# Loading q and k as whole tokens and transposing them on VectorE in an attention and two-MLP kernel

## The chip, the cores and the metric

The kernel runs on one core of a Trainium2 chip. The metric is the device time of one execution in microseconds (us), from three timed runs and one profiled execution. A core has a matrix engine (PE; PEld is its weight load), a vector engine (DVE), a scalar engine (ACT), a general engine (POOL) and a queue engine (SP) that issues the transfers here.

## The reference

```python
scores = scale * np.matmul(q, k.transpose(0, 1, 3, 2))    # 4 batches, 8 heads, 576 tokens, 64 features
masks = [mask_plain if h < H // 2 else mask_dil for h in range(H)]
scores = np.where(masks[None], scores, -1e9)
attn = exp(scores - max) / (sum + 1e-9)
x = matmul(attn, v)                                       # then to (4 * 576) tokens x 512
h = x @ w_in;  x = np.maximum(0.01 * h, h) @ w_out        # 512 -> 2048 -> 512
a = x @ w1;  b = x @ w2;  out = ((a * b) @ w3) @ w_out2    # 512 -> 1024 -> 1024 -> 512
```

The plain mask of heads 0 to 3 keeps the last 32 keys, the dilated one of heads 4 to 7 every fourth of the last 128. The weights are double precision.

## The kernel before

**Work and tiles.** Heads are taken in pairs, four a batch, two dilated and then two plain; a pair's work is cut into two parts r, so there are 32 steps n of attention. `x` of a batch feeds the first MLP in chunks c of 320 and 256 tokens: `hidden(c, f)` multiplies by the weight block `win` f into PSUM (`ps_h`), ACT takes the leaky unit (`g`), DVE and POOL or DVE split the result in a high and a low half (`gs`), and `project` multiplies by `wout` f into `ps_x`, two turns f later (`LAG = 2`). Each product is three matmuls (`mm3`, L112 to L114). After chunk 4 comes a folding of the last two weight matrices, and at the end the gated layer (`ps_ab`) and the output (`ps_y`).

**Weights.** While batch 0's attention runs, 32 blocks of double precision weights (`raw0` to `raw31`, win and wout in turn) are fetched by SP and converted by POOL (L103), ACT (L143, L145) and DVE (L146, L147), and split (L107, L108). Block 26 makes win 13.

**q and k.** `load_qk(m)` fetches q (m even) or k (m odd) of a pair: two transfers (L244), one for each head, with 6 (plain) or 8 (dilated) tokens a partition on 96 or 72 partitions, so that the two heads of a token stand side by side in pieces of 64 features, 256 bytes each. `transpose_qk(m)` turns the tile with 6 or 8 PE transposes (L306) in two groups of 3 or 4, each group into one PSUM bank, and DVE copies each bank to `qT` (L309, with the scale) or `kT` (L311) in the order of tokens that the masks want. `scores(n)` multiplies blocks of 64 queries by 96 keys (L328), DVE adds the mask (L336) and takes the maximum (L338), ACT the exponential (L341); `normalize`, `transpose_p` (L371) and `values` (L389) follow.

**Buffers.** Tiles of batch 0 (m below 8) have memory of their own in the place of weights; from batch 1 on all q and k tiles share the tag `nat` with two buffers, so a load waits until the tile two before it has been turned. `qT` and `kT` have two buffers each. Scores, values and the transposes of later batches share two PSUM banks (`side_bank`).

**Order.** A scheduler orders the instructions of each engine from the program's order and its own estimate of times; SP's order is kept by hand while the weights are fetched. `attention` calls, in step n, `transpose_p(n)`, `normalize(n+1)`, `scores(n+2)`, `transpose_qk(n+4)`, `load_qk(n+6)`, `values(n)`; `pace` interleaves these steps with the turns of the MLP.

Of the kernel before, what the change touches and what calls it, by code (L numbers as in the profile page):

```python
# [8 lines left out]
F32 = mybir.dt.float32  # L9
# [8 lines left out]
ALU = mybir.AluOpType  # L18
# [4 lines left out]
DILATION = 4  # L23
# [5 lines left out]
def tile_window_attention_two_mlps(  # L29
# [14 lines left out]
    nc = tc.nc  # L44
    P = 128
    B, H, S, D = q.shape
    T, DM = out.shape
    F1 = w_in.shape[1]
    F2 = w1.shape[1]
    SCALE = 1.0 / float(D) ** 0.5  # L50
    NC = DM // P
    NF = F1 // P
# [7 lines left out]
    SR = S // DILATION  # L60
# [4 lines left out]
    HP = H // 2  # L65


    def pool(name, side):
        es = ExitStack()
        return es, es.enter_context(  # L70
            tc.tile_pool(name=name, bufs=1, side=side, reuse_waits="tile")
        )
# [3 lines left out]
    win_es, win_p = pool("win", "left")  # L76
# [11 lines left out]
    def side_bank(name):  # L88
        return psum.tile([P, 512], F32, tag="side", name=name, bufs=2)

    def bank(name):
        return psum.tile([P, 512], F32, tag="h", name=name, bufs=2)
# [26 lines left out]
    def rows(t, off, dims):  # L119
        return bass.AP(t.tensor, t.offset + off, dims)  # L120
# [67 lines left out]
    win, wout, w12, wo2, wp = {}, {}, {}, {}, {}  # L188
# [26 lines left out]
    nat_t, v_t, qk_t, xs = {}, {}, {}, {}  # L215


    order, seq = [], []
# [7 lines left out]
    def pair(pi):  # L226
        b, h0 = divmod(pi, HP)
        return b, 2 * h0, 2 * h0 < H // 2

    def load_qk(m):  # L230
        if m >= 2 * NPAIR:
            return
        pi, nm = seq[m // 2], "qk"[m % 2]
        b, h0, plain = pair(pi)
        c = 6 if plain else 8
        n = S // c
        if m < 2 * HP:
            t = win_p.tile([P, 8, 2, D], F32, tag="win", name=f"{nm}{pi}", bufs=NF)
        else:
            t = att.tile([P, 8, 2, D], F32, tag="nat", name=f"{nm}{pi}", bufs=2)  # L240
        src = q if nm == "q" else k
        o = (b * H + h0) * S * D
        for j in range(2):
            nc.sync.dma_start(  # L244
                t[:n, :c, j, :], rows(src, o + j * S * D, [[c * D, n], [D, c], [1, D]])
            )
        nat_t[nm, pi] = t
# [5 lines left out]
    def first_key(i, plain):  # L253
        k0 = max(i * QB - WINDOW, 0)
        g0 = i * QB // SR * SR
        return k0 if plain else max(k0, g0)
# [31 lines left out]
    def transpose_qk(m):  # L288

        if m >= 2 * NPAIR:  # L290
            return
        pi, nm = seq[m // 2], "qk"[m % 2]
        plain = pair(pi)[2]
        c = 6 if plain else 8
        n = S // c
        t = nat_t.pop((nm, pi))
        dst = att.tile([P, S], F32, tag=nm + "T", name=f"{nm}T{pi}", bufs=2)
        if plain:
            to = dst.rearrange("d (p g c) -> d g c p", g=2, p=n)
        else:  # L300
            to = dst.rearrange("d (c p g) -> d g c p", g=2, p=n)
        for g in range(2):
            ps = (bank if m < 2 * HP else side_bank)(f"ps_{nm}T{pi}_{g}")
            for c1 in range(c // 2):
                src = t[:n, g * (c // 2) + c1].rearrange("p j d -> p (j d)")
                nc.tensor.transpose(ps[:, c1 * n : (c1 + 1) * n], src, ident[:n, :n])  # L306
            src = ps[:, : S // 2].rearrange("d (c p) -> d c p", p=n)
            if nm == "q":
                nc.vector.tensor_scalar(to[:, g], src, SCALE, None, op0=ALU.mult)  # L309
            else:  # L310
                nc.vector.tensor_copy(to[:, g], src)  # L311
        qk_t[nm, pi] = dst

    sm = {}
# [1 line left out]
    def scores(n):  # L316
        if n >= NR:
            return
        pi, r = order[n]
        plain = pair(pi)[2]  # L320
        qt, kt = qk_t["q", pi], qk_t["k", pi]
        bl = R_BLOCKS[r]
        nb = len(bl)
        ps = side_bank(f"ps_s{n}")[:, : nb * KB].rearrange("p (i k) -> p i k", k=KB)
        for i in bl:
            for j in range(2):
                d = slice(j * D, (j + 1) * D)
                nc.tensor.matmul(  # L328
                    ps[j * QB : (j + 1) * QB, i - bl.start],
                    qt[d, i * QB : (i + 1) * QB],  # L330
                    kt[d, first_key(i, plain) : first_key(i, plain) + KB],
                    start=True, stop=True,
                )
        s = att.tile([P, NQ, KB], F32, tag="s", name=f"s{n}", bufs=3)[:, :nb]
        mk = mask_p[:, NQ - nb :] if plain else mask_d[:, bl.start : bl.stop]
        nc.vector.tensor_tensor(s, ps, mk, op=ALU.add)  # L336
        nmax = att.tile([P, NQ], F32, tag="nmax", name=f"nmax{n}", bufs=2)
        nc.vector.tensor_reduce(nmax[:, :nb], s, op=ALU.max, axis=AX.X, negate=True)  # L338
        total = att.tile([P, NQ], F32, tag="total", name=f"total{n}", bufs=2)
        for i in range(nb):  # L340
            nc.scalar.activation(  # L341
                s[:, i], s[:, i], AF.Exp, bias=nmax[:, i : i + 1], accum_out=total[:, i : i + 1]
            )
        sm[n] = (s, total[:, :nb])
# [84 lines left out]
    def attention(n0, n1):  # L429

        for n in range(n0, n1):
            if n == N_EARLY:
                for m in range(NA, NA + 2):
                    load_qk(m)
                load_v(4)
                for m in range(NA, n + 4):
                    transpose_qk(m)
                    load_qk(m + 2)
                load_v(5)
# [3 lines left out]
            if n % 8 != 3:  # L443
                scores(n + 2)
                yield
            if n >= N_EARLY or n + 4 < NA:
                transpose_qk(n + 4)
            if n >= N_EARLY:
                load_qk(n + 6)
            yield  # L450
            if n % 8 == 3:
                scores(n + 2)
                yield
# [186 lines left out]
    with ExitStack():  # L640
        make_identity(nc, ident)
        att_es, att = pool("att", "right")
# [54 lines left out]
        with tc.manual_schedule(engines={mybir.EngineType.SP}):  # L697


            first = attention(0, N_EARLY)  # L700
            for x in "0aM1bFF2cFF3dFFFFXAAAAAAAAAAAACCCCCCCC":
                if x in "0123":
                    load_qk(2 * int(x))
                    load_qk(2 * int(x) + 1)
                elif x in "abcd":
                    load_v("abcd".index(x))
                elif x == "M":
                    build_masks()
                elif x == "X":
                    transpose_qk(0)  # L710
                    transpose_qk(1)
                    scores(0)
                    scores(1)
                    transpose_qk(2)
                    normalize(0)
                    transpose_qk(3)
                elif x == "A":
                    step(first, first)
                elif x == "F":
                    conv.fetch()  # L720
                else:
                    conv.step()
            step(*[first] * 10)
# [169 lines left out]
```

## Time and profile before

| what | value |
|---|---|
| timed runs | 916.11, 917.04, 918.66 us; median 917.04 |
| span of the profiled execution, first to last instruction | 916.2 us (no other time of that execution is given; its span lies 0.8 us under the median of the runs) |
| busy PE, DVE, ACT, POOL | 880.8, 345.9, 354.5, 247.8 us |
| transfers | 110938 packets, 95.94 MB |

The page gives busy time per engine, the span in 40 slices, the chain of work that ended last, and groups of instructions by line. A share of the whole span mixes stages: up to about 113 us weights are converted, from 113 to 355 us the PE transposes of q and k run between matmuls of the first MLP, and later stages have none of them. So the sums are made from windows and from the order of time.

### The profile page before, as it was taken

What the parts mean: (1) busy time and instruction counts of PE and PEld (TensorE: products, weight loads), DVE (VectorE), ACT (ScalarE), POOL (GpSimd) and SP (SyncE); (2) the same over time, 40 slices, a digit from 0 to 9 for tenths busy, and PEclk for the clock granted to TensorE, in tenths of its full rate; (3) what the DMA queues carried; (4) which work ended last, traced back from release to release, by engine and by line L of the source; (5) the groups of instructions that cost most, each with busy time, mean ns of one, the idle gap of its engine ahead of it and who ended that gap; (6) DMA issues with size and microseconds to landing.
All of it is one profiled execution on the core that took longest, in us unless ns stands there. A gap on an engine that the chain in (4) does not pass through costs nothing.

```text
span 916.2 us, 16026 instructions
## 1 busy us (share of the span) xinstructions
PE 880.8 (96%) x6456; PEld 832.4 (91%) x6456; DVE 345.9 (38%) x699; ACT 354.5 (39%) x904; POOL 247.8 (27%) x288
## 2 busy tenths in 40 slices
PE   4869899999999999999999999999999999999998
PEld 4658799999999999999999999999999998999997
DVE  4999864444333233264334345851101010100000
ACT  3898742433333333365333245742212121211211
POOL 3454410012222223254222143432213031211110
PEclk9559999999999999999999999999999999999999
DMA  7995502322213102177788665620101010000000
GB/s 170 313 271 129 180 19 57 83 48 73 49 44 78 45 14 62 47 252 282 235 293 271 211 201 160 202 79 1 46 24 35 35 35 24 12 24 12 12 24 35
DMA packets 110938, 95.94 MB, mean 105 GB/s; under 512 B 69520, under 2 KB 94352, under 8 KB 110864
## 3 DMA queue, kind: packets, MB, share of 16 engines
q1 hardware_dynamic: 110864, 94.92, 34.8%
q8 instruction: 51, 0.84, 0.4%
q14 instruction: 23, 0.19, 0.1%
HBM read 78.51 MB, written 16.38 MB: 104 GB/s over the span
## 4 chain that ended last, share of the span: by engine, by line
PE 82%; DVE 6%; ACT 3%; DMA 3%; SPq 2%; issue 2%; POOL 1%; DVEq 0%; POOLq 0%; ACTq 0%
PE ps_ab L112 7%; PE ps_ab L114 7%; PE ps_ab L113 7%; PE ps_h L113 6%; PE ps_h L114 6%; PE ps_x L112 6%; PE ps_h L112 6%; PE ps_x L114 6%; PE ps_x L113 6%; PE ps_y L113 4%; PE ps_y L112 4%; PE ps_y L114 4%; PE ps_s L328 2%; PE ps_o L389 2%; PE ps_wp L114 2%
## 5 line engine op out<-in xcount | busy, mean ns | idle before, releaser
L112 PE MATMUL ps_h<-x,win 128*128 128x320 f32 (+1 forms) x512 | 154.7, 303 | 3.6 <-DMA v<-in_v_dram 2.3
L113 PE MATMUL ps_h<-x,win 128*128 128x320 f32 (+1 forms) x512 | 155.4, 304 | 1.1 <-DVE x L422 1.1
L113 PE MATMUL ps_x<-gs,wout 128*128 128x320 f32 (+1 forms) x512 | 152.8, 299 | 2.4 <-DVE gs L108 2.4
L114 PE MATMUL ps_h<-x,win 128*128 128x320 f32 (+1 forms) x512 | 154.4, 302 | 0.0
L112 PE MATMUL ps_x<-gs,wout 128*128 128x320 f32 (+1 forms) x512 | 152.1, 299 | 1.1 <-DVE x L509 1.1
L114 PE MATMUL ps_x<-gs,wout 128*128 128x320 f32 (+1 forms) x512 | 152.7, 299 | 0.0
L112 PE MATMUL ps_ab<-ys,w 128*128 128x384 f32 x384 | 130.1, 339 | 0.0
L114 PE MATMUL ps_ab<-ys,w 128*128 128x384 f32 x384 | 130.0, 339 | 0.0
L113 PE MATMUL ps_ab<-ys,w 128*128 128x384 f32 x384 | 130.0, 338 | 0.0
L616 DVE TENSOR_TENSOR ab<-a,ps_ab 128x384 f32<-128x384 f32 x48 | 26.6, 554 | 253.0 <-ACT a L614 247.9
L107 DVE CAST gs<-g 128x320 fp32r<-128x320 f32 (+1 forms) x128 | 49.7, 391 | 153.6 <-ACT g L473 153.4
L108 POOL TENSOR_TENSOR p<-ab,p 128x384 fp32r<-128x384 f32 x48 | 48.5, 1011 | 218.6 <-ACT p L107 218.6
L108 POOL TENSOR_TENSOR gs<-g,gs 128x320 fp32r<-128x320 f32 (+1 forms) x80 | 66.4, 831 | 145.2 <-DVE gs L107 145.2
L112 PEld LDWEIGHTS ps_h<-x,win 128*128 128x128 f32 x512 | 97.9, 192 | 5.3 <-ACT x L420 4.2
L113 PEld LDWEIGHTS ps_x<-gs,wout 128*128 128x128 f32 x512 | 96.9, 189 | 3.8 <-DVE gs L108 2.9
L113 PEld LDWEIGHTS ps_h<-x,win 128*128 128x128 f32 x512 | 98.3, 192 | 2.1 <-DVE x L422 1.3
L112 PEld LDWEIGHTS ps_x<-gs,wout 128*128 128x128 f32 x512 | 96.5, 189 | 2.6 <-DVE x L509 1.3
L114 PEld LDWEIGHTS ps_h<-x,win 128*128 128x128 f32 x512 | 98.4, 192 | 0.3
L114 PEld LDWEIGHTS ps_x<-gs,wout 128*128 128x128 f32 x512 | 96.9, 189 | 0.5
L473 ACT ACTIVATE g<-ps_h 128x320 f32<-128x320 f32 (+1 forms) x128 | 51.4, 403 | 115.2 <-PE ps_h L114 114.1
L614 ACT COPY a<-ps_ab 128x384 f32<-128x384 f32 x48 | 23.0, 480 | 143.9 <-PE ps_ab L114 143.9
L112 PEld LDWEIGHTS ps_ab<-ys,w 128*128 128x128 f32 x384 | 72.0, 188 | 1.2
(91 smaller groups left out, 1514.8 us busy)
## 6 DMA issues: line engine op xcount, KB each, us to landing
wo<-wo_dram SPq DMA_DIRECT2D x32, 512.0 KB
raw<-in_moe_w_in_dram SPq DMA_DIRECT2D x16, 512.0 KB
raw<-in_moe_w_out_dram SPq DMA_DIRECT2D x16, 512.0 KB
rawf<-in_moe_w_dram SPq DMA_DIRECT2D x16, 512.0 KB
raww<-in_moe_w_dram SPq DMA_DIRECT2D x16, 512.0 KB
v<-in_v_dram SPq DMA_DIRECT2D x60, 96.0 KB
q<-in_q_dram SPq DMA_DIRECT2D x32, 144.0 KB
k<-in_k_dram SPq DMA_DIRECT2D x32, 144.0 KB
```

Source lines behind the costliest of these rows:

```text
L107: copy_on(e_hi)(hi, src)
L108: e_lo.tensor_tensor(lo, src, hi.bitcast(F32), op=ALU.subtract)
L112: nc.tensor.matmul(ps, a[1], b[0], start=first, stop=False)
L113: nc.tensor.matmul(ps, a[0], b[1], start=False, stop=False)
L114: nc.tensor.matmul(ps, a[0], b[0], start=False, stop=last)
L328: nc.tensor.matmul(ps[j * QB : (j + 1) * QB, i - bl.start], qt[d, i * QB : (i + 1) * QB], kt[d, first_key(i, plain) : first_key(i, plain) ...
L389: nc.tensor.matmul(ps[j * D : (j + 1) * D, i * QB : (i + 1) * QB], vt[i][:, h + j, :], t[:, i, j * QB : (j + 1) * QB], start=True, stop=True,)
L473: nc.scalar.activation(g, ps, AF.Prelu, alpha=SLOPE)
L614: nc.scalar.copy(t, ps[0][:, :TB])
L616: nc.vector.tensor_tensor(g, t, ps[1][:, :TB], op=ALU.mult)
```

## The change

For batches 1 to 3 (m from 8 on) `load_qk` calls `load_halves`: four transfers, each to 32 partitions; partition p of a quarter takes 18 consecutive tokens of one head with all features, 1120 numbers in one run of 4480 bytes. Quarters 1 and 3 start 32 features later, so the first 32 numbers of every 64 in a partition are the half of the features that its quarter needs, and the others aren't used. `turn_halves` transposes on DVE in blocks of 32 x 32: one instruction for a plain tile (18 blocks), four for a dilated one (5, 5, 4, 4 blocks), written straight to `qT` or `kT`. No PE transpose, no PSUM bank and no copy is left for these m. Batch 0 keeps its transposes, with a plain copy for q and k alike. The scale moves to the mask: one instruction with two operations where one addition stood.

```diff
+    def load_halves(m, src, o):
+        t = att.tile([P, NT, D], F32, tag="nat", name=f"{nm}{pi}", bufs=2)
+        for g in range(P // E):
+            og = o + g // 2 * S * D + g % 2 * E
+            to = t[g * E : (g + 1) * E]
+            x = NT * D - E
+            nc.sync.dma_start(
+                to.rearrange("p n d -> p (n d)")[:, :x], rows(src, og, [[NT * D, E], [1, x]])
+            )
+    def turn_halves(m):
+        dst = att.tile([P, S], F32, tag=nm + "T", name=f"{nm}T{pi}", bufs=2)
+        if pair(pi)[2]:
+            nc.vector.transpose(dst.rearrange("d (r n) -> d n r", n=NT), t[:, :, :E])
+        else:
+            for v in range(DILATION):
+                us = len(range(v, NT, DILATION))
+                other = (NT + v) % DILATION * SR + (NT + v) // DILATION
+                to = bass.AP(
+                    dst.tensor, dst.offset + v * SR,
+                    [list(dst.ap[0]), [1, us], [2 * NT // DILATION, E // 2], [other - v * SR, 2]],
+                )
+                at = bass.AP(
+                    t.tensor, t.offset + v * D,
+                    [list(t.ap[0]), [DILATION * D, us], [2, E // 2], [1, 2]],
+                )
+                nc.vector.transpose(to, at)
...
-            if nm == "q":
-                nc.vector.tensor_scalar(to[:, g], src, SCALE, None, op0=ALU.mult)
-            else:
-                nc.vector.tensor_copy(to[:, g], src)
+            nc.vector.tensor_copy(to[:, g], src)
...
-        nc.vector.tensor_tensor(s, ps, mk, op=ALU.add)
+        nc.vector.scalar_tensor_tensor(s, ps, SCALE, mk, op0=ALU.mult, op1=ALU.add)
```

Three places in the order of instructions show what moves. The first is PE after the scores of step 14 (`ps_s14`), where the turns of q 10 begin; before:

```order
L114 MATMUL ps_x1_0_0_1495<-gs1_14_2181,wout14_1633 128x256
L328 MATMUL ps_s14_2136<-kT4_1808,qT4_1686 64x96 x8
L306 MATMUL ps_qT10_0_2185<-ident_80,q10_1941 128x72 x4
L112 MATMUL ps_x1_0_1_1496<-gs1_14_2181,wout14_1633 128x256
L113 MATMUL ps_x1_0_1_1496<-gs1_14_2181,wout14_1633 128x256
```

The group at L306 is gone from PE in the changed kernel, as are all groups of m from 8 on. On DVE, behind the mask of the same step, before (each L309 copies one PSUM bank):

```order
L336 TENSOR_TENSOR s14_2145<-ps_s14_2136,masks_89 128x384
L309 TENSOR_SCALAR qT10_2184<-ps_qT10_0_2185 128x288
L338 TENSOR_REDUCE nmax14_2147<-s14_2145 128x4
L350 TENSOR_SCALAR total14_2149<-total14_2149 128x4
L353 RECIPROCAL rec14_2255<-total14_2149 128x4
L107 CAST gs0_9_2371<-g0_9_2369 128x320
L309 TENSOR_SCALAR qT10_2184<-ps_qT10_1_2191 128x288
```

and there in the changed kernel:

```order
L265 STREAM_TRANSPOSE qT10_2136<-q10_1898 128x5x16x2 x2
L265 STREAM_TRANSPOSE kT10_2252<-k10_1970 128x5x16x2 x2
L376 TENSOR_REDUCE nmax14_2099<-s14_2097 128x4
L460 TENSOR_TENSOR x1_0_2157<-ps_o12_2146,x1_0_2157 128x320
L265 STREAM_TRANSPOSE qT10_2136<-q10_1898 128x4x16x2
L265 STREAM_TRANSPOSE kT10_2252<-k10_1970 128x4x16x2
L265 STREAM_TRANSPOSE qT10_2136<-q10_1898 128x4x16x2
L265 STREAM_TRANSPOSE kT10_2252<-k10_1970 128x4x16x2
L388 TENSOR_SCALAR total14_2101<-total14_2101 128x4
L391 RECIPROCAL rec14_2201<-total14_2101 128x4
L107 CAST gs1_15_2187<-g1_15_2185 128x256
```

q and k of a pair are now turned together, eight instructions close behind one another, and the next `gs` cast stands after all of them. The third place is SP's queue while the last weights are fetched, before:

```order
L244 DMA q4_954<-in_q_dram 96x6x64 x2
L127 DMA raw26_1216<-in_moe_w_in_dram 128x4x128
L124 DMA raw27_1228<-in_moe_w_out_dram 128x512
L244 DMA k4_1173<-in_k_dram 96x6x64 x2
L127 DMA raw28_1284<-in_moe_w_in_dram 128x4x128
```

and in the changed kernel:

```order
L242 DMA q4_938<-in_q_dram 32x1120 x4
L242 DMA k4_1151<-in_k_dram 32x1120 x4
L242 DMA q5_1668<-in_q_dram 32x1120 x4
L242 DMA k5_1783<-in_k_dram 32x1120 x3
L127 DMA raw26_1196<-in_moe_w_in_dram 128x4x128
L124 DMA raw27_1208<-in_moe_w_out_dram 128x512
```

The fetches of raw 26 to 31 moved behind the loads of k4, q5 and k5; those of q5 and k5 wait for the transposes of q4 and k4 on DVE, since `nat` has two buffers.

## Rows read from the trace of the kernel before

**Rows 1.** The page: span, and busy time, share and instructions of each engine.
```profile
span 916.2 us, 16026 instructions
PE 880.8 (96%) x6456; PEld 832.4 (91%) x6456; DVE 345.9 (38%) x699; ACT 354.5 (39%) x904; POOL 247.8 (27%) x288
```
**Rows 2.** Windows by stage: busy time of each engine (with instructions), granted clock, transfer share.
```profile
core 0: us, PE busy (x) PEld busy (x) DVE busy (x) ACT busy (x) POOL busy (x), PEclk, DMA share, GB/s
63.00:93.00 30.00, 27.84 (x204) 26.10 (x204) 29.82 (x54) 23.89 (x51) 13.04 (x14) 0.92 0.64 163
105.00:108.00 3.00, 0.92 (x4) 0.47 (x4) 3.00 (x4) 3.00 (x7) 3.00 (x3) 1.00 1.03 404
108.00:111.00 3.00, 2.69 (x25) 2.47 (x26) 2.97 (x7) 3.00 (x7) 1.30 (x2) 0.61 0.69 161
113.00:355.00 242.00, 242.00 (x2300) 233.12 (x2299) 96.56 (x241) 86.21 (x310) 49.66 (x58) 1.00 0.22 53
```
**Rows 3.** A window of line L306 alone, the PE transposes of q and k.
```profile
113.00:355.00 242.00, 16.75 (x136) 13.20 (x134) 1.00 0.22 53
```
**Rows 4.** PE in order of time around one group: start us, length us, instruction.
```profile
144.70 0.28 PE L113 MATMUL ps_x<-gs,wout 128*128 128x256 f32 x1
144.82 0.28 PE L114 MATMUL ps_x<-gs,wout 128*128 128x256 f32 x1
144.95 0.41 PE L306 MATMUL ps_qT<-ident,q 96*128 96x96 f32 x3
145.14 0.36 PE L112 MATMUL ps_h<-x,win 128*128 128x256 f32 x1
145.34 0.28 PE L113 MATMUL ps_h<-x,win 128*128 128x256 f32 x1
```
**Rows 5.** The same view behind scores, without and with a group.
```profile
142.45 1.04 PE L328 MATMUL ps_s<-kT,qT 64*64 64x96 f32 x20
...
143.65 0.28 PE L113 MATMUL ps_x<-gs,wout 128*128 128x256 f32 x1
...
214.55 1.04 PE L328 MATMUL ps_s<-kT,qT 64*64 64x96 f32 x20
215.52 0.47 PE L306 MATMUL ps_qT<-ident,q 96*128 96x96 f32 x3
...
216.00 0.31 PE L112 MATMUL ps_h<-x,win 128*128 128x320 f32 x1
```
**Rows 6.** DVE groups by shape, and two copies in order of time (dilated, plain).
```profile
L336 DVE TENSOR_TENSOR s<-ps_s,masks 128x480 f32<-128x480 f32 x16 | 10.4, 652 | 18.4 <-PE ps_s L328 18.4
...
L336 DVE TENSOR_TENSOR s<-ps_s,masks 128x384 f32<-128x384 f32 x16 | 8.8, 553 | 15.6 <-PE ps_s L328 15.6
...
64.73 0.45 DVE L309 TENSOR_SCALAR qT<-ps_qT 128x288 f32<-128x288 f32 x1
...
216.21 0.69 DVE L309 TENSOR_SCALAR qT<-ps_qT 128x288 f32<-128x288 f32 x1
```
**Rows 7.** Transfers, 134 to 140 us (k alone), then 396 to 402 us (rows of 4096 bytes).
```profile
q1 hardware_dynamic: 1184, 0.30, 21.7%
...
q1 hardware_dynamic: 456, 1.66, 87.9%
```
**Rows 8.** SP's queue in order of time: start, length, transfer issued.
```profile
94.19 0.40 SPq L127 DMA_DIRECT2D raw<-in_moe_w_in_dram  x1
...
99.01 1.26 SPq L244 DMA_DIRECT2D k<-in_k_dram  x2
```
**Rows 9.** DVE in order of time: the mask of step 9.
```profile
97.91 0.54 DVE L336 TENSOR_TENSOR s<-ps_s,masks 128x384 f32<-128x384 f32 x1
```
**Rows 10.** Groups from `ps_h` to `gs` of 256-token chunks: busy us, mean ns, idle before.
```profile
L473 ACT ACTIVATE g<-ps_h 128x256 f32<-128x256 f32 x64 | 23.9, 376 | 46.1 <-PE ps_h L114 45.9 <-ACT w L107 0.2
...
L107 DVE CAST gs<-g 128x256 fp32r<-128x256 f32 x64 | 24.2, 381 | 63.0 <-ACT g L473 62.9
...
L108 DVE TENSOR_TENSOR gs<-g,gs 128x256 fp32r<-128x256 f32 x32 | 17.5, 548 | 0.7
```

More of the change, by code (lines that the diff above doesn't have):

```diff
@@ L228, in pair @@
         return b, 2 * h0, 2 * h0 < H // 2
+    E = 32
+    NT = S // E
+    def load_halves(m, src, o):
+        pi, nm = seq[m // 2], "qk"[m % 2]
+        t = att.tile([P, NT, D], F32, tag="nat", name=f"{nm}{pi}", bufs=2)
[6 more added lines that the diff above has]
+            )
+        nat_t[nm, pi] = t
+    def turn_halves(m):
+        pi, nm = seq[m // 2], "qk"[m % 2]
+        t = nat_t.pop((nm, pi))
+        dst = att.tile([P, S], F32, tag=nm + "T", name=f"{nm}T{pi}", bufs=2)
[14 more added lines that the diff above has]
+                nc.vector.transpose(to, at)
+        qk_t[nm, pi] = dst
     def load_qk(m):
@@ L236, in load_qk @@
         n = S // c
-        if m < 2 * HP:
-            t = win_p.tile([P, 8, 2, D], F32, tag="win", name=f"{nm}{pi}", bufs=NF)
-        else:
-            t = att.tile([P, 8, 2, D], F32, tag="nat", name=f"{nm}{pi}", bufs=2)
         src = q if nm == "q" else k
         o = (b * H + h0) * S * D
+        if m >= 2 * HP:
+            load_halves(m, src, o)
+            return
+        t = win_p.tile([P, 8, 2, D], F32, tag="win", name=f"{nm}{pi}", bufs=NF)
         for j in range(2):
@@ L292, in transpose_qk @@
         pi, nm = seq[m // 2], "qk"[m % 2]
+        if m >= 2 * HP:
+            turn_halves(m)
+            return
         plain = pair(pi)[2]
@@ L302, in transpose_qk @@
         for g in range(2):
-            ps = (bank if m < 2 * HP else side_bank)(f"ps_{nm}T{pi}_{g}")
+            ps = bank(f"ps_{nm}T{pi}_{g}")
             for c1 in range(c // 2):
@@ L307, in transpose_qk @@
             src = ps[:, : S // 2].rearrange("d (c p) -> d c p", p=n)
-            if nm == "q":
-                nc.vector.tensor_scalar(to[:, g], src, SCALE, None, op0=ALU.mult)
-            else:
-                nc.vector.tensor_copy(to[:, g], src)
+            nc.vector.tensor_copy(to[:, g], src)
         qk_t[nm, pi] = dst
```

## The prediction

> **What bounds the kernel now.** I read the page's busy times first: PE 96% of the span, no other engine above 39% [rows 1]. A busy PE can still be waiting inside, so I went to windows by stage. From 113 to 355 us PE is busy without a hole at full granted clock (1.00, the 2.4 GHz level), while DVE has 96.6 us of 242, POOL 49.7, and transfers 0.22 of their time [rows 2]. There, whatever is taken from PE comes off the end, as long as the engines behind it keep up. Ahead of it the picture is another: from 63 to 93 us DVE is full (29.8 of 30) and PE is nearly so (27.8) [rows 2]. There a longer DVE can show. One more row matters there: from 105 to 108 us PE is busy for 0.9 of 3 us, and in the next 3 us the granted clock is 0.61, partly the 1.2 GHz level [rows 2]; a hole on PE costs more than itself.
>
> **PE, steady stage.** The change removes 24 tiles' transposes, 12 plain with 6 and 12 dilated with 8: 168. Of these 136 stand in the window 113 to 355 us, 16.75 us of busy time [rows 3]. That is not the gain, because pipelined instructions overlap. I take starts instead. Matmuls of 256 columns start 0.12 us apart (144.70, 144.82); across a group of three transposes it takes 144.82 to 145.34, 0.52 us for two starts instead of 0.24: 0.28 us a group [rows 4]. Behind scores: from the first score to the second matmul after, 1.20 us without a group and 1.45 with one, less 0.03 since the second case has 320 columns: 0.22 to 0.23 [rows 5]. The 136 are 24 groups of three and 16 of four: 40 groups at 0.22 to 0.28 are 8.8 to 11.2 us. I take **10.3**, nearer the upper end, for the clean place is the one with least else in it; 16.75 stays as the outer bound.
>
> **DVE, per tile.** A transpose of 32 x 32 blocks doesn't occur in the trace. Adding the mask takes 652 ns for 480 and 553 for 384 elements: 1.03 ns an element and 0.16 us for the instruction [rows 6]. That is the lower bound: a plain tile (576 elements, one instruction) 0.75 us, a dilated one (four instructions) 1.22. The upper bound comes from the copies: 288 elements take 0.45 us where they are written 8 bytes apart (dilated), 0.69 where 24 bytes apart (plain) [rows 6], which is (0.69 - 0.16) / 288 = 1.85 ns an element. The transposes write 72 bytes apart or to two far places in turn, so that row is nearer: 1.22 plain, 1.69 dilated. The copies removed are 2 x 0.69 = 1.38 and 2 x 0.45 = 0.90 a tile. Per tile that is -0.2 (plain) and +0.8 (dilated) by the value I take, -0.6 and +0.3 by the lower.
>
> The rows show that a wider step on the write side makes a DVE instruction dearer. The Trainium skill, SBUF — State Buffer, section "Door 1: The DMA port swizzle", says that accesses inside one 16-byte line run at full rate and that each crossing to a new line pays; 8 against 24 bytes agrees with that. By it the dearer price would hold for all 24 tiles, by a flat price the cheaper; the difference is about 11 us of DVE time over the program, most of it where DVE is idle six tenths of the time.
>
> In the steady stage this is hidden. What covers it: `project` stands two turns behind `hidden`, 2 x 24 matmuls x 0.12 = 5.8 us [rows 4], of which ACT and DVE need 0.38 + 0.38 + 0.55 = 1.3 [rows 10]. So DVE may stand up to 4.5 us in a transposing stretch before PE misses `gs`; a dilated pair, q and k together, takes 2.4 to 3.4. If the cover were gone, each pair would cost PE the excess.
>
> **DVE, early stage.** m 8 to 11 (dilated) and 12, 13 (plain) fall before or about 113 us, with DVE full: 4 x 0.8 - 2 x 0.2 = +2.8 us at my price, 0 at the lower. Against it PE loses eight groups there, 8 x 0.28 = 2.2 us, and the turns no longer need a PSUM bank. I enter **+0.5**, between -2.2 and +2.8.
>
> **SP and transfers.** Before, a k tile is 1184 packets, 21.7% of 16 engines for 6 us: 20.8 engine-us, 1.3 us on all 16 [rows 7]. The new tile has 128 runs of 4480 bytes. In the other window 456 packets, nearly all of 4096 bytes, take 84.4 engine-us, 0.185 us each [rows 7]; scaled by bytes 0.20, so 128 are 26 engine-us, 1.6 us, though twice the bytes move. At a share of 0.22 that costs nothing. Issuing takes 0.63 us a transfer [rows 8]; four are at most 2.5 us of a queue with long pauses.
>
> What does move is the fetch of raw 26 to 31, which now queues on SP behind q5 and k5. These wait for the DVE transposes of q4 and k4, which stand just behind the mask of step 9, at 97.9 us before [rows 9]. So raw 26 leaves at about 98 + 4 (the two transposes, 2.4, and the DVE work between) + 4 (seven issues of 0.6), some 105 us, where it left at 94.2 and only k4 stood behind it, at 99.0 [rows 8]. On POOL the normalizing of step 10, on DVE the mask of step 10 and the first `gs` cast of chunk 1 stand behind block 26's conversion, and PE waits for those. Win 13 itself is wanted only at turn 13 of chunk 1. Cost 0 to 4 us, less the 4.5 us of lag: **+0.5**.
>
> The scale in the mask instruction: one pass over the same elements; I enter 0, and bound it by 32 x 0.16 = 5 us of DVE time, hidden after 113 us, under 2 us before.
>
> **Sum.** -10.3 + 0.5 + 0.5 = -9.3. Against the span, 916.2 gives 906.9; the span lies 0.8 us under the median, so **907.5** for the median of runs.
>
> **Rivals.**
> 1. The early stage loses. DVE at its dearer price and the late raw fetches leave holes on PE; a hole drops the clock as at 105 us. 2.8 + 3 + about 1.2 at the lower clock = 7 us instead of 1: 913.7, and 911 to 916 about it. For: DVE is full there. Against: the lag, and PE's own eight groups less.
> 2. The early stage gains. PE is the later one there and loses its waits for banks: -11.2 - 2.2 - 1 gives about 902; with all busy time of the groups, 16.75, it is 900.
> 3. **Slower.** The DVE transposes are far dearer than any copy here. A pair (2c) blocks DVE longer than 4.5 us and PE waits for `gs` each time, ten pairs after 113 us. It decides from 10 x (2c - 4.5) = 9.3, c = 2.7 us a tile, 4.4 ns an element; at c = 3.5, 25 us are lost, and the early tiles add 4 x 2.6 = 10: 942. For: the operation is not in the trace, its writes are scattered. Against: 1.85 ns is the dearest element in rows 6.
> 4. No change, 917: the removed groups filled places where PE would wait for `gs` or PSUM anyway. Against: 242.0 of 242 us busy with even starts.
>
> The Trainium skill's page VectorE: DVE Perf Modes ("Rules for kernel authors") advises TensorE for a 128 x 128 transpose where PSUM may be the destination; that speaks for rival 3, and no row here shows it, since the trace has no DVE transpose.
>
> **How the numbers follow.** Forecast 0.62 (903 to 911), rival 1 0.14, rival 2 0.12, rival 3 0.07, rival 4 0.05. The range 900 to 914 holds the forecast and rival 2 and part of rival 1, about 0.8. Runs of this kernel can't tell less than about 0.3% (2.8 us) from no change: faster is below 914.3. Faster: 0.62 + 0.12 + 0.09 of rival 1 = 0.83; same: 0.05 of rival 1 and rival 4, 0.10; slower: rival 3, 0.07.
>
> **What would show it.** The stage without holes should shrink by about 10 us, PE still full and L306 down to 56 instructions. The DVE transposes should take about 1.2 us plain and 0.3 to 0.5 each of four dilated. PE's waits for `gs` should stay near zero after 113 us. SP should show raw 26 leaving after 100 us, and POOL or ACT waiting for it a few us. The forecast fails if DVE transposes run over 2.7 us a tile, or if the stretch without holes begins later than about 117 us.

## The result and the profile after

The changed kernel takes **903.56 us** (median; 902.71 to 904.68) where the kernel before took 916.85 (916.11 to 918.66): ratio 0.985, 95% interval 0.9835 to 0.9865. The profiled execution has a span of 902.0 us and a time of its own of 903.77, so 14.2 us of span went, 13.3 us by the medians. (Here an execution's time is about 1.8 us over its span, so the span of 916.2 us before belongs to an execution of about 918.0 us, a little slow for that kernel.) The page after, first the span, then busy time of each engine, answers to [rows 1]:

```profile
span 902.0 us, 15754 instructions
PE 867.0 (96%) x6288; PEld 817.8 (91%) x6288; DVE 356.3 (40%) x711; ACT 352.3 (39%) x904; POOL 252.1 (28%) x288
```

PE has 168 instructions and 13.8 us of busy time less; its idle time, 35.4 us before, is 35.0 now. So over the whole span the gain lies in what PE does, not in how long it waits; the early stage, further down, is less simple. DVE has 10.4 us more. Windows by stage, against [rows 2] (us, then busy time of each engine with instructions, granted clock, transfer share, GB/s):

```profile
core 0: us, PE busy (x) PEld busy (x) DVE busy (x) ACT busy (x) POOL busy (x), PEclk, DMA share, GB/s
63.00:93.00 30.00, 27.53 (x213) 25.43 (x214) 30.00 (x66) 22.92 (x49) 12.30 (x13) 0.92 0.81 226
105.00:108.00 3.00, 2.00 (x25) 1.72 (x23) 2.61 (x6) 2.49 (x9) 0.27 (x1) 1.00 0.00 0
108.00:111.00 3.00, 2.47 (x18) 2.27 (x19) 2.68 (x8) 3.00 (x10) 0.81 (x2) 1.00 0.99 304
113.00:130.00 17.00, 15.81 (x129) 15.09 (x130) 15.13 (x27) 11.02 (x24) 6.53 (x7) 1.00 0.21 69
130.00:343.00 213.00, 213.00 (x2027) 204.05 (x2028) 90.24 (x222) 77.62 (x296) 46.55 (x56) 1.00 0.32 80
```

Between 130 and 343 us PE is full in both kernels, so a window can't show the gain there: the work moved forward instead. What shows it is the time at which a chunk of the first MLP is done, the DVE copy of its `ps_x`. For the fourth of the eight chunks, in order of time (start us, length us, instruction, idle time before), the kernel before and then the changed one:

```profile
342.60 0.69 DVE L509 COPY x<-ps_x 128x512 f32<-128x512 f32 x1 [1.03 <-PE ps_x L114]
```

```profile
329.90 0.68 DVE L547 COPY x<-ps_x 128x512 f32<-128x512 f32 x1
```

It is a fair mark, since PE has started nearly the same work by then in every kernel below: 1556 to 1558 large matmuls, 524 of the scores, 122 transposes of probabilities. Two things differ. Of the 48 old groups, three are still to come where the late ones exist. And some kernels have 488 value matmuls behind them instead of 468; twenty take 0.7 to 0.8 us (ten of them hold PE from 139.82 to 140.21 in the changed kernel), and the column of leads allows 0.7. So the changed kernel leads by 12.7 + 0.7 = **13.4 us** there. On the span it leads by 14.2: the three groups come to it later. From the profiled executions, with medians and ratios from all runs:

| kernel | fourth chunk done, us | lead there, us | lead at the end, us | median, us | ratio to before [95%] |
|---|---|---|---|---|---|
| before | 342.60 | | | 916.85 | |
| changed | 329.90 | 13.4 | 14.2 | 903.56 | 0.985 [0.9835, 0.9865] |
| e1_scale_only | 342.41 | 0.2 | -0.9 | 917.38 | 1.0 [0.9991, 1.0009] |
| e2_turn_twice | 332.39 | 10.9 | 12.4 | 905.54 | 0.9863 [0.9847, 0.988] |
| e11_turn_four | 351.03 | -7.7 | -7.1 | 923.92 | 1.006 [1.0041, 1.0079] |
| e3_pe_groups_kept | 340.94 | 1.7 | -1.8 | 918.07 | 1.0004 [0.9994, 1.0015] |
| e5_from14 | 335.02 | 8.3 | 7.0 | 909.80 | 0.9911 [0.9896, 0.9925] |
| e6_only8to13 | 337.93 | 4.7 | 4.3 | 914.13 | 0.9956 [0.9938, 0.9973] |
| e7_before_h_banks | 343.20 | -0.6 | -2.6 | 919.58 | 1.0022 [1.0009, 1.0035] |
| e8_banks_taken | 329.32 | 14.0 | 15.5 | 902.78 | 0.9832 [0.9817, 0.9846] |
| e9_groups_8to13 | 332.62 | 10.7 | 8.7 | 908.27 | 0.9892 [0.9876, 0.9907] |
| e12_groups_and_copies | 334.23 | 9.1 | 8.8 | 907.09 | 0.989 [0.987, 0.991] |
| e10_pace1 | 330.72 | 12.6 | 13.1 | 905.32 | 0.9874 [0.9857, 0.989] |
| e10_owed2 | 329.02 | 14.3 | 15.8 | 901.92 | 0.9835 [0.982, 0.985] |

A second pair of marks bounds the late part, the same copy of the second chunk, before and after:

```profile
172.33 0.69 DVE L509 COPY x<-ps_x 128x512 f32<-128x512 f32 x1
```

```profile
168.87 0.68 DVE L547 COPY x<-ps_x 128x512 f32<-128x512 f32 x1
```

From the second chunk's copy to the fourth's, 170.3 us before and 161.0 after, PE is never idle and never at half clock in either kernel. Of the 9.2 us between them, 16 scores, 9 transposes of probabilities and 2 large matmuls more in the kernel before take about 2 us (an estimate, by starts in these traces of about 0.05, 0.1 and 0.12 us each). Some 7 us are left for 27 groups of PE transposes, 0.26 each.

The new operation, groups of DVE by shape (busy us, mean ns of one, idle before), with the mask beside it:

```profile
L374 DVE SCALAR_TENSOR_TENSOR s<-ps_s,masks 128x480 f32<-128x480 f32 x16 | 10.4, 653 | 12.1 <-PE ps_s L366 11.8
...
L252 DVE STREAM_TRANSPOSE qT<-q 128x576 f32<-128x576 f32 x6 | 7.5, 1247 | 0.0
L252 DVE STREAM_TRANSPOSE kT<-k 128x576 f32<-128x576 f32 x6 | 7.4, 1239 | 0.4 <-DMA k<-in_k_dram 0.4
...
L265 DVE STREAM_TRANSPOSE kT<-k 128x128 f32<-128x128 f32 x12 | 4.8, 399 | 0.0
L265 DVE STREAM_TRANSPOSE kT<-k 128x160 f32<-128x160 f32 x12 | 4.7, 459 | 0.6 <-DMA k<-in_k_dram 0.6
```

A plain tile takes 1.24 us, a dilated one 2 x 0.46 + 2 x 0.40 = 1.72; DVE waited 1.0 us in all for their loads. The mask with its scale takes what it took alone, 653 against 652 ns [rows 6].

### The profile page after: what moved, and what is told of

Its sections match the earlier page's. It is cut to its first block, busy times and chain, and to the rows that moved or that the text cites. A ratio compares the mean times of both kernels' runs of the same rounds, so it can differ in the third digit from the quotient of the medians.

```text
span 902.0 us, 15754 instructions
## 1 busy us (share of the span) xinstructions
PE 867.0 (96%) x6288; PEld 817.8 (91%) x6288; DVE 356.3 (40%) x711; ACT 352.3 (39%) x904; POOL 252.1 (28%) x288
## 4 chain that ended last, share of the span: by engine, by line
PE 83%; DVE 4%; DMA 3%; issue 1%; POOL 1%; ACT 1%; SPq 0%; DVEq 0%; POOLq 0%; ACTq 0%
PE ps_ab L112 8%; PE ps_ab L114 8%; PE ps_ab L113 8%; PE ps_x L112 7%; PE ps_x L113 6%; PE ps_x L114 6%; PE ps_h L114 6%; PE ps_h L113 6%; PE ps_h L112 6%; PE ps_y L113 4%; PE ps_y L112 4%; PE ps_y L114 4%; PE ps_s L366 2%; PE ps_o L427 2%; PE ps_wp L114 2%; PE ps_wp L113 2%
## 5 line engine op out<-in xcount | busy, mean ns | idle before, releaser
L113 PE MATMUL ps_h<-x,win 128*128 128x320 f32 (+1 forms) x512 | 153.2, 299 | 3.0 <-DVE x L460 3.0
L112 PE MATMUL ps_h<-x,win 128*128 128x320 f32 (+1 forms) x512 | 153.2, 300 | 2.2 <-ACT x L458 1.8
L114 PE MATMUL ps_h<-x,win 128*128 128x320 f32 (+1 forms) x512 | 152.8, 298 | 0.0
L107 DVE CAST gs<-g 128x320 fp32r<-128x320 f32 (+1 forms) x128 | 53.7, 421 | 161.2 <-ACT g L511 161.1
```

Of the source, the lines that this page charges most:

```text
L107: copy_on(e_hi)(hi, src)
L112: nc.tensor.matmul(ps, a[1], b[0], start=first, stop=False)
L113: nc.tensor.matmul(ps, a[0], b[1], start=False, stop=False)
L114: nc.tensor.matmul(ps, a[0], b[0], start=False, stop=last)
```

## Experiments on the scale and on VectorE's cover

**The scale alone**, in the kernel before:

```diff
-            if nm == "q":
-                nc.vector.tensor_scalar(to[:, g], src, SCALE, None, op0=ALU.mult)
-            else:
-                nc.vector.tensor_copy(to[:, g], src)
+            nc.vector.tensor_copy(to[:, g], src)
-        nc.vector.tensor_tensor(s, ps, mk, op=ALU.add)
+        nc.vector.scalar_tensor_tensor(s, ps, SCALE, mk, op0=ALU.mult, op1=ALU.add)
```

> The kernel before with the scale moved into the mask's instruction and a plain copy for q, and nothing else of the change. My theory: the scale costs and gives nothing, 917 us (916 to 918). Rival: part of the 13 us comes from the scale, through a shorter copy of q or another order: 914 or less.

Measured 917.38 us beside 917.42 for the kernel before, with an interval of 0.8 us either way: no part of the result that could be seen comes from here.

**VectorE's transposes done twice, then four times over** (each loop stands around both calls):

```diff
-            nc.vector.transpose(dst.rearrange("d (r n) -> d n r", n=NT), t[:, :, :E])
+            for _ in range(2):
+                nc.vector.transpose(dst.rearrange("d (r n) -> d n r", n=NT), t[:, :, :E])
-                nc.vector.transpose(to, at)
+                for _ in range(2):
+                    nc.vector.transpose(to, at)
```

> The changed kernel with every transpose on VectorE written twice, so 12 x 1.24 + 12 x 1.72 = 35.5 us more of VectorE work. My theory: behind 120 us VectorE has room and the lag of two turns covers it, so only the six tiles of the early stage show, 9.4 us of extra work in a stage where VectorE is full: 905 to 912 us, 908 likeliest. Rival: VectorE's transposes are on the path everywhere (a pair, now 5 to 7 us, is longer than the 4.5 us of cover): 925 to 939 us.

> The changed kernel with each VectorE transpose done four times over: some 6 us of VectorE time a tile instead of 1.2 to 1.7, about 107 us more in all (35.5 us for the doubled ones, times three). Where does the cover end that the prediction put at 4.5 us a pair? Theory of the prediction: a pair blocks VectorE in one piece, and TensorE misses gs for what lies over 4.5 us: twelve pairs of 10 to 13.8 us, ten of them where TensorE is full, 5 x 9.3 + 5 x 5.5 = 74 us, some 977. Rival: the scheduler spreads the transposes between the gs casts, and only what VectorE can't do in the stage's idle time costs; between 130 and 343 us it is busy for 90 of 213 us, so 80 us more still fit; the early tiles (six of them, 4.4 us each more than now, where VectorE is full) cost up to 26 us: 906 to 930. Between 935 and 970 both would be at work.

Twice: 905.54 us, 2 us more than the changed kernel (the intervals of the two ratios overlap) for 35.5 us more of DVE. Four times: 923.92, 20.4 us more for about three times as much. Windows of the run with four (columns as above):

```profile
113.00:130.00 17.00, 15.08 (x134) 13.71 (x132) 17.00 (x32) 12.65 (x31) 6.67 (x7) 1.00 0.77 225
130.00:343.00 213.00, 203.35 (x1887) 193.01 (x1887) 146.51 (x351) 70.78 (x270) 43.27 (x51) 0.98 0.33 78
```

In 130 to 343 us PE is idle for 9.65 us, not for the 74 that blocks of a whole pair would cost. DVE in order of time, same run, shows why (a plain pair):

```profile
205.14 1.23 DVE L253 STREAM_TRANSPOSE kT<-k 128x576 f32<-128x576 f32 x1
206.21 0.31 DVE L107 CAST gs<-g 128x320 fp32r<-128x320 f32 x1
206.45 1.23 DVE L253 STREAM_TRANSPOSE qT<-q 128x576 f32<-128x576 f32 x1
207.52 1.24 DVE L253 STREAM_TRANSPOSE kT<-k 128x576 f32<-128x576 f32 x1
208.60 0.47 DVE L108 TENSOR_TENSOR gs<-g,gs 128x320 fp32r<-128x320 f32 x1
209.00 2.52 DVE L253 STREAM_TRANSPOSE kT<-k 128x576 f32<-128x576 f32 x2
211.36 0.31 DVE L107 CAST gs<-g 128x320 fp32r<-128x320 f32 x1
211.59 0.64 DVE L376 SCALAR_TENSOR_TENSOR s<-ps_s,masks 128x480 f32<-128x480 f32 x1
```

The scheduler puts the casts of `gs` between the transposes, so a pair is no single block. And where PE does wait in that stage (113 to 343 us; total, times, longest), it is mostly for the mask of the attention step, not for `gs`:

```profile
PE ps_p L411 <- DVE s L376: 5.6, 3, 4.0
PE ps_x L113 <- DVE gs L108: 2.6, 4, 0.9
PE ps_p L411 <- DVE x L462: 1.4, 2, 1.0
```

So the rival with the scheduler's spreading held, and the "block" theory fell. The test has a limit: four transposes leave gaps between them that one instruction four times as long would not, and no run has such an instruction. Of the 21.1 us lost by the fourth chunk (351.03 against 329.90), 13.8 stand already at the second (182.67 against 168.87), where the six tiles of m 8 to 13 meet a full DVE. A part of both is the clock: PE stood at half speed from 101.6 to 111.8 us and again from 210.8 to 217.6 us.

## Experiments on the PE groups

**All 48 groups of PE transposes put back**, from the new tile into a bank that nobody reads (the loop stands at the head of `turn_halves`; their output is left unread):

```diff
+        c = 6 if pair(pi)[2] else 8
+        n, flat = S // c, t.rearrange("p n d -> p (n d)")
+        for g in range(2):
+            ps = side_bank(f"ps_{nm}T{pi}_{g}")
+            for c1 in range(c // 2):
+                x = (g * (c // 2) + c1) * P
+                nc.tensor.transpose(ps[:, c1 * n : (c1 + 1) * n], flat[:n, x : x + P], ident[:n, :n])
```

> The changed kernel with the 48 groups of PE transposes put back beside VectorE's, from the same tiles into PSUM banks that nobody reads: 168 transposes of the old shapes. It tells what the groups alone cost. My theory: 0.22 to 0.28 us a group, 48 groups, 10.6 to 13.4 us: 914 to 917 us. Rival 1: they fill places where PE would wait anyway: 904 to 906 us. Rival 2: they cost their whole busy time and more, 17 to 21 us: 921 us or more.

918.07 us, just over the 914 to 917 of my theory: the whole gain is gone with PE's groups back, although loads, DVE transposes and scale are all as changed. By the fourth chunk, 45 groups had cost 13.4 - 1.7 = 11.7 us, 0.26 each; another 4.3 us of span came behind that mark, where only three groups are left. For those there is no account, except that the profiled execution, 919.77 us, was the slowest of ten.

**The change for m from 14 on alone, and for m 8 to 13 alone** (the other tiles go the old way):

```diff
-        if m >= 2 * HP:
+        if m >= 14:
```

```diff
-        if m >= 2 * HP:
+        if 8 <= m < 14:
```

> The change for m from 14 on alone; m 8 to 13, whose tiles fall into the stage up to 120 us, stay as before (two transfers, PE transposes, copies), and the order of the early stage is that of the kernel before. The 18 tiles are 36 groups on PE. Theory A: a group is worth 0.22 to 0.28 us in the full stretch, 8 to 10 us in all, and the other 4 us came from the early stage: 907 to 909 us. Theory B: the early stage gave nothing and the groups behind it are worth about 0.35 us each: 904 to 905 us.

> The change for m 8 to 13 alone, the six tiles up to about 120 us; m from 14 on as before. It is the other half of the run with m from 14 on, which left 909.8. Theory A: the two halves add up, and this one is worth 903.6 - 909.8 = -6 against the kernel before, of which 12 groups on PE are 3 us and the rest is the early stage: 911 to 912 us. Theory B: it is worth its 12 groups alone, 914 us, and the missing 3 us come from both together.

909.80 and 914.13 us. The fourth chunk's copy, first with m from 14 on, then with m 8 to 13:

```profile
335.02 0.68 DVE L551 COPY x<-ps_x 128x512 f32<-128x512 f32 x1
```

```profile
337.93 0.68 DVE L551 COPY x<-ps_x 128x512 f32<-128x512 f32 x1
```

With the 0.7 us of values in the first, the leads are 8.3 us for 33 late groups (0.25 each) and 4.7 for the 12 early ones (0.39 each); together 13.0, nearly the 13.4 of the whole change. By the medians it is 7.6 and 3.7, so 11.3 of 13.3, and 914.13 us is the figure of theory B; with intervals of some 1.5 us on each, the medians don't tell the two theories apart. So the early tiles, entered at no gain, bring about a third of the gain. What they bring beyond their 12 groups (some 3.1 us at 0.257) is less sure: against the kernel before it is 1.6 us by the fourth chunk and 0.6 by the medians, against the kernel with m from 14 on alone 2.0 and 3.1.

**The 12 early groups put back, unread; then with their copies too:**

```diff
-        for g in range(2):
+        for g in range(2 if m < 14 else 0):
```

```diff
+            nc.vector.tensor_copy(dst[:, g * S // 2 : (g + 1) * S // 2], ps[:, : S // 2])
```

(The first line changes the loop of the edit above; the second stands behind its transposes, and DVE's own transposes overwrite the copy.)

> The changed kernel with the PE groups of m 8 to 13 alone put back, into side banks that nobody reads: 12 of the 48 groups. With all 48 it was 918.1, 14.5 us more than without. If every group costs alike, 0.30 us, this is 903.6 + 3.6 = 907.2 us. If the early ones cost more, through the banks and the hole at 105 us, and the later ones 0.22 to 0.28: 908 to 911 us. If they hide in the early stage's waits: 904 to 905 us.

> The changed kernel, with the PE groups of m 8 to 13 put back and each bank copied by VectorE into the tile before the transposes overwrite it (twelve groups, twelve copies of 0.45 to 0.69 us, some 7 us of VectorE time, all before 120 us). Theory: what the early stage gained, beyond the PE time of the groups, is that a bank is no longer held until a copy comes up in VectorE's full queue, and scores and values behind it no longer wait for that bank. Then this kernel gives back what the old path for those m gave back: 909.5 to 912, some 2 to 3 us more than the 908.3 of the groups alone. Rival: the groups cost by their PE time only, and the copies add VectorE work that is covered, as the doubled transposes were: 908 to 909. Second rival: VectorE's time alone decides in the early stage; 7 us more where it is full would give 912 to 915.

908.27 and 907.09 us. By the fourth chunk, groups alone, then groups and copies:

```profile
332.62 0.68 DVE L554 COPY x<-ps_x 128x512 f32<-128x512 f32 x1
```

```profile
334.23 0.68 DVE L555 COPY x<-ps_x 128x512 f32<-128x512 f32 x1
```

The groups cost 2.7 us, 0.23 each; part of it is the clock, which stood at half speed from 113.6 to 117.0 us in this run and nowhere from 68 to 900 us in the changed kernel. With the copies, which took 0.45 us each and 5.1 in all instead of the 7 expected, it is 4.3, near the 5.1 of the old path (335.02 against 329.90), as the theory of the bank held in DVE's queue would have it. But the whole runs show no loss by the copies: the median of 907.09 is under all that was expected, and its interval overlaps that of 908.27. In the two profiled executions (909.23 and 909.32) that is because the run without copies lost 1.7 us more behind that mark (the last point of this document shows where). So, by the mark, the groups on PE bring back about half of what the early tiles gained, with the waits and the clock that came along; where the other 2 us are from isn't settled.

**What a bank does.** Two runs: the old kernel with banks of another pool for the early groups, and the changed kernel with the side banks taken in turn for nothing:

```diff
-            ps = (bank if m < 2 * HP else side_bank)(f"ps_{nm}T{pi}_{g}")
+            ps = (bank if m < 14 else side_bank)(f"ps_{nm}T{pi}_{g}")
```

```diff
+        for g in range(2 if m < 14 else 0):
+            nc.vector.memset(side_bank(f"ps_{nm}T{pi}_{g}")[:, :8], 0.0)
```

> The kernel before with one word changed: the PE transposes of m 8 to 13 go to the PSUM banks of tag h, which the first MLP's hidden products use, instead of the two side banks that scores and values use. Theory (banks): in the early stage the transposes hold up scores and values through the side banks, so that the values of step 7, which chunk 1 waits for, come at 105 us, PE has a hole and its clock falls; without that 1.5 to 4 us are gained: 913 to 915.5 us. Rival: the order of banks does nothing: 916.5 to 918 us; or hidden is held up instead: over 918 us.

> The changed kernel with the side banks still taken in turn for m 8 to 13: two tiny writes of VectorE to side banks ahead of each tile's transposes, and no work of PE. Theory (banks): a part of what the early stage gained goes again: 905 to 907 us. Rival: the banks' turn costs nothing without the PE groups: 903 to 904.5 us.

919.58 and 902.78 us. Taking the banks costs nothing. In the other kernel the hole at 105 us is gone, but `hidden` is held up earlier (windows, columns as above):

```profile
63.00:93.00 30.00, 26.83 (x185) 23.64 (x185) 29.32 (x56) 23.61 (x51) 12.15 (x13) 0.78 0.66 163
...
105.00:108.00 3.00, 3.00 (x35) 2.69 (x34) 3.00 (x5) 2.57 (x5) 1.83 (x2) 1.00 1.05 383
```

185 matmuls from 63 to 93 us at a mean clock of 0.78 stand against 204 at 0.92 [rows 2]. It moved the trouble, so it proves nothing about the banks either way.

## Experiments on the order of the early stage

**Pace and weights let in** (attention at 1 a turn; weight blocks at 2 a step):

```diff
-                owed[0] += 1.25 if turn < 8 else 0
+                owed[0] += 1 if turn < 8 else 0
```

```diff
-                    owed_w[0] += 1.75
+                    owed_w[0] += 2
```

> The changed kernel, with attention steps let in at 1 instead of 1.25 a turn for the first eight turns of the MLP. Theory that the raw fetches behind q5 and k5 cost the early stage about 1.3 us (the holes up to 118 us): fewer attention steps early bring raw 26 to 31 forward and the holes shrink, 901.5 to 903; if the holes come from VectorE being full whatever the order, the time stays at 903 to 904.5; if attention becomes the late one, 905 to 907.

> The changed kernel, with weight blocks let in at 2 instead of 1.75 a step, so that raw 26 to 31 stand earlier in SP's queue, ahead of k4, q5 and k5. Theory that the late raw fetches cost about 1.3 us: 901.5 to 903. If VectorE is the limit up to 118 us and conversion work only changes places with attention work: 903 to 905.

905.32 us: slower pacing gains nothing (1.8 us more than the changed kernel as medians, with overlapping intervals), although raw 26 left SP at 95.94 instead of 98.15 and raw 28 at 104.11 instead of 106.99. 901.92 for the weights: 1.6 us less than the changed kernel as medians, with overlapping intervals, so no sure gain. Nor did it do what it was meant to: raw 26 leaves SP at 98.98, not before the 98.15 of the changed kernel, and its lead on the changed kernel at the fourth chunk is 0.9 us. So the one run with earlier fetches, in which attention came later too, wasn't faster; whether they would help by themselves stays open.

## Why the prediction held, and which term was off

The predicted time was 907.5 in 900 to 914, the measured one 903.56: the direction and the main reason held, 4 us more were gained than forecast, nearer to rival 2's 902. Two slips at the end of the sum are small: 906.9 and 0.8 are 907.7, and the 0.8 sets one execution's span against the times of others, where span and time of the same execution differ by 1.8 (902.0 and 903.77). The steps in turn:

**PE, steady stage.** Right. A group was entered at 0.257 us; the late ones gave 0.25, those put back 0.23 and 0.26, and the stretch from the second to the fourth chunk 0.26. For the 36 groups from m 14 on that is 9.3 us expected and 9.0 at the measured 0.25. Both places from which the price was read, [rows 4] at 0.28 and [rows 5] at 0.22, bracket it; busy time [rows 3] is refuted as a price.

**DVE's price.** The dearer end was right to 2%: 1.24 and 1.72 us, expected 1.22 and 1.69. From the plain tile (1.24 - 0.16) / 576 = 1.87 ns an element, as for the copy written 24 bytes apart (1.85). The Trainium skill's rule on crossings of 16-byte lines (SBUF — State Buffer, "Door 1: The DMA port swizzle") agrees with both: 24 and 72 bytes apart cost the same, 8 bytes apart less. That the step of the writes sets the price of the transposes is not shown, since no transpose with a dense destination ran; the price met may be the operation's own.

**The cover.** That these transposes are hidden after 113 us held (PE is full from 130 to 343 us); the 4.5 us that a pair might take did not. By that figure, twelve pairs of four transposes each would have cost some 74 us, and 20 were lost. Rival 3, decided by the same figure from 2.7 us a tile on, was priced wrongly for the same reason: at about 6 us a tile, in four or more pieces, the kernel is 0.6% slower than before, not 942 us or more.

**DVE, early stage: the term that was mis-sized.** Entered at +0.5, within -2.2 and +2.8, and with the late fetches +1.0. The early tiles alone gave a lead of 4.7 by the fourth chunk. First, DVE's 2.8 us were charged in full because DVE was full there [rows 2]; doubling all its transposes showed that a full DVE in this stage doesn't pass its work on to PE one to one (9.4 us more on the early tiles, 2.5 us by the fourth chunk). PE's relief was in the sum about rightly: 12 groups, some 3.1 us over the two terms. The run that put them back lost 2.7, but with 3.4 us at half clock in it, so it doesn't isolate that price. Second, PE's holes in this stage were taken as they stood, and several went. In the kernel before, PE in order of time (idle before, and what ended it):

```profile
105.72 0.50 PE L112 MATMUL ps_h<-x,win 128*128 128x256 f32 x2 [1.16 <-ACT x L420]
106.72 0.42 PE L371 MATMUL ps_p<-ident,s 128*96 128x128 f32 x2 [0.50 <-ACT pT L373]
108.31 1.55 PE L328 MATMUL ps_s<-kT,qT 64*64 64x96 f32 x20 [1.17 <-DVE x L422]
```

The first and the third of these are waits for the values that end batch 0: ACT writes the high half of their `x` at 105.30, and DVE takes the low half from the same bank at 107.85, which frees the bank for the scores; after, DVE does so at 96.76. In the changed kernel these waits are gone, and with them the stretch at half clock: the granted clock is 1.00 from 108 to 111 us, where it was 0.61 [rows 2]. Half speed lasted from 108.7 to 112.1 us before, 3.4 us, so about 1.7 us of matmul time. That looks like the 2 us that are left, but the kernel with the change for m 8 to 13 alone speaks against it. It has lost the same waits, stands at half clock from 109.4 to 112.8 us, as long as the kernel before, and still leads by 4.7 us (windows of that kernel):

```profile
93.00:105.00 12.00, 11.35 (x96) 10.81 (x95) 10.76 (x20) 8.10 (x23) 4.71 (x5) 1.00 0.52 139
108.00:111.00 3.00, 2.74 (x19) 2.46 (x20) 3.00 (x5) 3.00 (x7) 2.66 (x2) 0.73 1.04 329
```

What both kernels share is fewer holes from 93 to 105 us. PE is idle there for 0.65 us in this kernel and 0.69 in the changed one, against 1.68 before (the kernel before, then the changed one):

```profile
93.00:105.00 12.00, 10.32 (x95) 9.24 (x94) 9.79 (x21) 8.89 (x23) 4.54 (x7) 1.00 0.47 141
```

```profile
93.00:105.00 12.00, 11.31 (x95) 10.77 (x94) 10.18 (x18) 7.49 (x21) 4.74 (x5) 1.00 0.66 190
```

Two of the holes before belong to the removed work itself: PE stands at a group of transposes until the mask has read the scores in that side bank, and at the next step until DVE has copied `kT` out of one. Such a wait comes back with the groups (in order of time, twice the kernel before, then the changed kernel with the early groups put back unread):

```profile
98.51 0.47 PE L306 MATMUL ps_kT<-ident,k 72*128 72x72 f32 x4 [0.80 <-DVE s L336]
102.06 0.50 PE L371 MATMUL ps_p<-ident,s 128*96 128x128 f32 x3 [0.43 <-DVE kT L311]
```

```profile
107.01 0.71 PE L257 MATMUL ps_qT<-ident,q 96*128 96x96 f32 x6 [1.85 <-DVE s L381]
```

That also fits the run that took the banks without PE work and lost nothing. But other waits of PE are longer in the changed kernel (from 105 to 130 us it is idle for 3.3 us, before for 2.4), so these holes are a part of the 2 us by argument only: no run separates waits, clock and order, and the rest stays open.

**SP and transfers.** The raw fetches did move behind q5 and k5, only less far. SP in the changed kernel, in order of time (start, length, transfer issued):

```profile
93.92 1.71 SPq L242 DMA_DIRECT2D q<-in_q_dram  x4
96.12 1.24 SPq L242 DMA_DIRECT2D k<-in_k_dram  x3
98.15 0.39 SPq L127 DMA_DIRECT2D raw<-in_moe_w_in_dram  x1
```

Raw 26 left at 98.2 instead of 94.2 [rows 8], not at 105: the mask of step 9, from which the estimate was counted, itself came at 90.4 instead of 97.9 [rows 9]. If this has a price, it is in the new holes that follow, in the changed kernel's PE, though all three end with work of DVE:

```profile
108.44 0.39 PE L112 MATMUL ps_x<-gs,wout 128*128 128x256 f32 x1 [1.44 <-DVE x L547]
...
112.24 0.39 PE L113 MATMUL ps_x<-gs,wout 128*128 128x256 f32 x1 [0.55 <-DVE gs L108]
...
117.15 0.39 PE L113 MATMUL ps_x<-gs,wout 128*128 128x256 f32 x1 [1.06 <-DVE gs L108]
```

PE is idle for 1.2 us between 113 and 130, where it was full before; what share of that the late fetches have isn't shown. The hole-free stretch begins after 117 us, which the prediction named as a sign of failure: the sign was badly chosen, since the work done by then was further on (300 large matmuls started by 120 us, 260 before).

**The rest of the span** got no entry. Its 1.5 us, 573.6 before and 572.1 after, are the 0.7 of values and three groups at 0.25. In other kernels the lead falls by up to 3.5 us behind the mark or grows by up to 1.5, though little but the order differs there; that is how far one profiled execution can be trusted for a cause.

**Rivals.** Rival 4 (no change) and rival 3 fell with the runs that kept the groups and multiplied the transposes. Rival 1 had the sign of the early stage wrong. Rival 2 (early stage gains) was right about that stage, with too high a price for the steady one (11.2 where 40 groups at 0.25 are 10.0). The Trainium skill's advice for a 128 x 128 transpose (VectorE: DVE Perf Modes, "Rules for kernel authors": TensorE, where PSUM may take the result) doesn't hold in this kernel: with PE full, 168 transposes kept on PE cost 14.5 us. The same tiles turned on a VectorE that is busy for 90 of 213 us cost little: doing them all twice took 2 us more.

## What to carry to other kernels

Where PE runs without a hole, price work that is taken off it by the starts of its neighbours, from more than one place (0.22 and 0.28 here, around a measured 0.25; busy time would say 0.42), and let a less loaded engine do it even if it is slower at it. A full engine in a stage is not yet the bound of that stage: ask which wait PE ends last there, and count PE's own relief and the waits that the removed work brought with it. Before a lower clock is made the cause of a loss, look for a run that has the one without the other. A cover worked out from one chain is a lower bound where a scheduler can put urgent instructions between the others.

## What the runs showed of the hardware

- A VectorE transpose in 32 x 32 blocks takes about 1.87 ns an element and partition with writes 72 bytes apart (1.24 us for 128 x 576, f32), and 0.40 and 0.46 us for 128 x 128 and 128 x 160: the price that a copy written 24 bytes apart has here.
- Multiplying by a scalar and adding in one instruction costs what the addition alone costs: 653 against 652 ns for 128 x 480.
- The length of a single hole on PE doesn't tell whether the clock falls: 2.06 us without work up to 107.36 us left it at 1.00 in the run that took the banks for nothing, and 1.59 us up to 108.26 us was followed by half speed from 109.4 us with the change for m 8 to 13 alone.
- A hole on PE late in the program can be followed by half clock too, and that moves with the order. With the early groups put back, from 403 to 408 us (windows, that kernel and then the changed one):

```profile
403.00:408.00 5.00, 4.34 (x23) 4.34 (x24) 2.94 (x6) 2.18 (x4) 2.10 (x3) 0.66 1.00 393
```

```profile
403.00:408.00 5.00, 5.00 (x44) 5.00 (x43) 0.86 (x3) 1.79 (x4) 1.48 (x2) 1.00 1.04 403
```

  23 matmuls instead of 44 in the same 5 us, with 0.66 us idle and half speed from 403.8 to 407.2 us: most of the loss is the clock, not the hole. The changed kernel has its hole there earlier, from 398 to 400 us (PE busy for 0.88 of 2), and keeps the full clock.
